# Linear attention and two gated networks on one core: the attention scores always multiplied by the decay on VectorE, straight from PSUM

## The chip, the cores and the metric

The kernel runs on one core of one Trainium2 chip. The metric is the device time of one execution in microseconds (us); lower is better. The engines are written as the profile writes them: PE (TensorE matmul), PEld (TensorE weight load), DVE (VectorE), ACT (ScalarE), POOL (GpSimd) and SP (SyncE, which issues the transfers).

## The reference, cut to what matters

Three stages follow one another. The first is a linear attention over 4 batches, 8 heads and 768 positions, in chunks, with a decay `a` per position:

```python
L = np.exp(cum[:, :, :, None] - cum[:, :, None, :]) * causal   # decay from j to i
CB = np.einsum('bhin,bhjn->bhij', Cc, Bc)                      # scores
M = CB * L                                                     # scores weighed by the decay
y = np.einsum('bhij,bhjd->bhid', M, xc) + y_inter              # y_inter comes from the running state
...
v = k * k @ w_v ;  r = sigmoid(xr @ w_r) ;  x = r * v          # second stage, with k = relu(xk @ w_k)
h = max(x @ w1, x @ w2, x @ w3) ;  out = h @ w_out             # third stage
```

The line `M = CB * L` is the one that the change is about. Here its tile is 128 x 128 per batch, head and block of 128 positions.

## The kernel before, in words

The positions are cut into 6 blocks of 128 (`t`), and the work of a block is: `attention(b, t)` for the 4 batches, then `gate` and `ffn` (the second stage, 512 tokens at a time, block 0 in two halves of 256), then `maxout` and `final` (the third stage). The attentions of block `t + 1` are handed in between `ffn` and `maxout` of block `t`. Large matmuls are made from a high and a low fp32r part of each operand, three products each (`three`, `mm3` at L599). The weights arrive in 64-bit form and are turned into such pairs on the chip, by `load_split` (L549): an absolute value on ACT (L558), four bit operations on DVE (L559 to L565), a copy for the high part (L366/L368) and a subtraction for the low part (L374). All of that falls into the first block.

In `attention(b, t)`, B, C and x are loaded into `bc` and `xt` (L624 to L627), B and C are transposed on PE into a PSUM bank (L641) and copied to `kT` (L645/L646). The decay tile `L` (8 heads x 128 x 128, a ring of two buffers `lr`, `cr` in the code) is loaded as rows by a DMA (L690), masked on POOL (L692) and made into exponentials on ACT (L701, or L697 and L705); for block 0 three of the four batches form it by matmuls (L660 to L684). The scores are made by `cb()` (L708, profile line L712) into four PSUM banks of the pool `pb` (`pa` for the first two batches), 256 columns each. Then they are multiplied by `L` into the SBUF tile `M`, four products of 128 x 256 per attention, 96 in all. At last `yt` (L749) multiplies `M` by x (L761), adds the state's part (L757), and makes the state's update (L752); results go to `xb` (L775/L776) and `st` (L782 to L786).

Each of the 96 products is made by the helper `weigh` (L601). It declares two operations. The first has two choices: DVE multiplies the scores in PSUM by `L` and writes `M` (profile line L604, DVE), or ACT copies the scores from PSUM to `M` (L604, ACT). The second is there only where ACT was chosen: POOL or DVE multiplies `M` by `L` within SBUF (L606).

The order of the work isn't the order of the code. `Plan` holds every operation with its costs by engine and what it depends on. `forward` (L115) goes through time: an engine that is free takes the ready operation with the smallest key. An operation with a choice of engines is put into each engine's queue, into DVE's with `spare` (200 or 1000 ns by turns, `SPARE`) added to its key, and into that of an engine named in `hold` only after so many ns:

```python
                for e in ([late] if late else costs):
                    if not late and e in hold:
                        heapq.heappush(pending, (now + hold[e], i, e))
                        ...
                    heapq.heappush(ready[e], (key[i] - ops[i][4] + (spare if len(costs) > 1 and e == "DVE" else 0.0), i))
```

So ACT gets a copy when DVE hasn't taken the product within 150 ns (`HOLD`). Forty rounds of this are made, with keys from the round before, and the shortest is issued. Each engine then executes its list in that order. Where PE would be idle before the last block-0 matmuls, small matmuls are put in to fill the time (profile line L988).

Of the kernel before, what the change touches and what calls it, by code (L numbers as in the profile page):

```python
# [11 lines left out]
AF = mybir.ActivationFunctionType  # L12
# [43 lines left out]
class Plan:  # L56
# [26 lines left out]
    def op(self, eng, cost, fn, r=(), w=(), after=(), issue=475.0, unless=None, hold=None, tail=0.0, lock=False):  # L83
        deps = set(after)
        for b in r:
            deps.update(b.writers)
        for b in w:
            deps.update(b.readers)
            deps.update(b.writers)
        i = len(self.ops)  # L90
        costs = eng if isinstance(eng, dict) else {eng: cost}
        self.ops.append((costs, fn, sorted(deps), issue, self.bias, unless, hold or {}, tail, lock))
        for b in w:
            b.writers = [i]
            b.readers = []
        for b in r:
            b.readers.append(i)
        return i
# [188 lines left out]

HALVES = (0,)
FIRST = 2
HOLD = 150.0  # L290
HOLD_L = 300.0
HOLD_COPY = 100.0
BIAS = (0.0, 0.0, 0.0)
# [5 lines left out]
def kernel(  # L299
# [20 lines left out]
    P = 128  # L320
# [30 lines left out]
    op = plan.op  # L351
    V, G, A, T, Q = nc.vector, nc.gpsimd, nc.scalar, nc.tensor, nc.sync
# [4 lines left out]
    def tt(n):  # L357
        return 68 + 1.042 * n

    def pool(n, narrow=False):  # L360
        return 147 + (1.95 if narrow else 2.11) * n
# [137 lines left out]
    for s in range(2):  # L499
        hs = halves[s]  # L500
        p = boot.next()
# [3 lines left out]
        p = boot.next()  # L505
# [5 lines left out]
    for s in range(2):  # L511
        p = boot.next()
# [22 lines left out]
    p = boot.next()  # L535
# [62 lines left out]
        for i, (l, r_) in enumerate(terms):  # L598
            T.matmul(pt, l, r_, start=(i == 0), stop=(i == last))  # L599

    def weigh(dst, src, by, n, r, rb, after):  # L601

        i = op({"DVE": tt(n), "ACT": 51 + 0.833 * n}, 0, lambda e: (
            V.tensor_mul(dst, src, by) if e == "DVE" else A.activation(dst, src, AF.Copy)),  # L604
            r=r + [rb], after=after, hold={"ACT": HOLD})
        return op({"POOL": pool(n), "DVE": tt(n)}, 0, lambda e: (V if e == "DVE" else G).tensor_mul(dst, dst, by),  # L606
                  r=[rb], after=[i], unless=(i, "DVE"), lock=True)


    def attention(b, t):  # L610
        ts = slice(t * P, (t + 1) * P)
# [5 lines left out]
        wide = boot if first and b < 2 else pc  # L617
        xb, b_xb = xbs[t % 2], b_xbs[t % 2][b]
        bc, xt, cr = bcr.next(), xtr.next(), lr.next()
# [30 lines left out]
        crg = [Buf(), Buf()]  # L650
        for g in range(2):
            cg = cr.ap[:, 4 * g:4 * g + 4, :]
            cc = ccol[:, qs][:, 4 * g:4 * g + 4, None].to_broadcast([P, 4, P])
            if parts:
                p = wide.next()
# [13 lines left out]
            elif not rows:  # L669
                p = wide.next()  # L670
# [16 lines left out]
            else:  # L687
# [7 lines left out]
                def shift(e, g=g, cg=cg, cc=cc):  # L695
# [3 lines left out]
                    for h in range(4):  # L699
# [3 lines left out]
                i = op({"DVE": tt(512), "POOL": pool(512), "ACT": 4 * 293}, 0, shift, r=[b_cc[b // 2], b_nc[b // 2]],  # L703
                       w=[crg[g]], hold={"ACT": HOLD_L}, lock=True)
# [9 lines left out]
        i = op("PE", 760, cb, r=[kT], w=wide.bufs)  # L714
# [4 lines left out]
        for g in range(2):  # L719
            m = mr.next()  # L720
            ms.append(m)
            base = list(m.readers) + list(m.writers)
            mw = [weigh(m.ap[:, 2 * k:2 * k + 2], wide.bufs[2 * g + k].ap[:, :2 * P].rearrange("p (s i) -> p s i", s=2),
                        cr.ap[:, 4 * g + 2 * k:4 * g + 2 * k + 2], 2 * P, [wide.bufs[2 * g + k]], crg[g], base) for k in range(2)]
            m.writers, m.readers = mw, []
            last.extend(mw)
        cr.readers = last
# [21 lines left out]
        def yt():  # L749
# [9 lines left out]
            for h in range(H):  # L759
# [4 lines left out]
        i = op("PE", (750 if first else 1250) + (170 if more else 0), yt,  # L764
               r=[*ms, xt] + ([] if first else [kT, b_st[b]]) + ([bd] if more else []), w=yb + ([p3] if more else []))
# [7 lines left out]
        base = list(b_xb.readers) + list(b_xb.writers)  # L773
# [4 lines left out]
        if more:  # L778
# [4 lines left out]
            else:  # L783
# [5 lines left out]
                   r=[u, b_dec], w=[b_st[b]], lock=True)  # L789
# [166 lines left out]

    plan.bias = BIAS[1]
    attention(0, 0)
    plan.bias = BIAS[2]
    attention(1, 0)  # L960
    plan.bias = 0.0
    weights_front()
    attention(2, 0)
    attention(3, 0)
    weights_back()
# [56 lines left out]
```

## Time and profile before

| | |
|---|---|
| median of 3 runs | 464.77 us (463.24 to 465.58) |
| the profiled execution's own time | 464.19 us |
| span of the profiled execution | 462.4 us, 8496 instructions |
| PE busy | 439.7 us (95%), 3210 instructions |
| PEld busy | 359.3 us (78%) |
| DVE busy | 287.2 us (62%), 574 instructions |
| ACT busy | 267.3 us (58%), 597 instructions |
| POOL busy | 114.0 us (25%), 140 instructions |
| mean granted TensorE clock | 0.984 of full speed |

The profiled execution's time is its span and 1.79 us around it. Engines work side by side, so their busy times don't add up to the span. A duration of a row is that of one instruction; where a row has several instructions behind one another (x2, x3), its time is that of the whole stretch, which shows at what pace they follow.

### The profile page before, as it was taken

The page shows a single profiled execution, that of the slowest core. Times are in us where ns is not written, and L with a number is a line of the kernel's source. Part 1 is how long each engine was busy: PE and PEld are TensorE (multiplying, and loading weights), DVE is VectorE, ACT ScalarE, POOL GpSimd, SP SyncE. Part 2 cuts the span into 40 slices and gives each one's busy share as a digit, 9 for nine tenths or more (in the row PEclk, how much of TensorE's full clock was granted, in tenths as well). Part 3 has the DMA queues.
Part 4 walks back from the last instruction along what each step waited for, and adds up shares of the span by engine and source line. Part 5 has one row for each costly group of instructions (what it writes and reads, how often), then busy time and mean ns, then how long its engine had stood idle before and what let it go on. Part 6 is the DMA issues. An engine that isn't in the chain of part 4 may idle for free.

```text
span 462.4 us, 8496 instructions
## 1 busy us (share of the span) xinstructions
PE 439.7 (95%) x3210; PEld 359.3 (78%) x3210; DVE 287.2 (62%) x574; ACT 267.3 (58%) x597; POOL 114.0 (25%) x140
## 2 busy tenths in 40 slices
PE   7759899987999999999999999999999999999997
PEld 7648788755887877887877887877888777888887
DVE  5898999979545469635459635459635448423441
ACT  6588999649574454584354584354584433673231
POOL 3022101042024335324335324334322313120000
PEclk9898989999899999999999999999999999999999
DMA  8875636724003342102342102342102400000001
GB/s 220 204 177 115 161 104 163 211 54 87 23 6 71 87 78 59 34 1 62 91 78 58 34 1 62 90 79 59 34 1 51 98 1 0 24 1 23 1 2 45
DMA packets 105705, 31.86 MB, mean 69 GB/s; under 512 B 77632, under 2 KB 101568, under 8 KB 105664
## 3 DMA queue, kind: packets, MB, share of 16 engines
q1 hardware_dynamic: 105664, 31.31, 29.4%
q8 instruction: 25, 0.41, 0.4%
q14 instruction: 16, 0.13, 0.1%
HBM read 27.91 MB, written 3.39 MB: 68 GB/s over the span
## 4 chain that ended last, share of the span: by engine, by line
PE 82%; DVE 7%; ACT 4%; DMA 3%; issue 2%; POOL 1%; SPq 0%; POOLq 0%; ACTq 0%
PE pa L599 47%; PE pa L880 13%; PE pa L936 10%; PE pb L712 2%; PE pb L761 2%; PE pb L641 2%; DMA bc<-in_C_dram 2%; PE pb L757 1%; ACT L L701 1%; DMA L<-crd 1%; PE pb L988 1%; DVE tmp L914 1%; PE pb L936 1%; PE pb L752 1%; DVE tmp L822 1%
## 5 line engine op out<-in xcount | busy, mean ns | idle before, releaser
L914 DVE TENSOR_TENSOR tmp<-tmp,pa 128x512 f32<-128x512 f32 x72 | 49.2, 685 | 45.7 <-PE pa L599 37.4
L374 DVE TENSOR_TENSOR k2l<-tmp,k2h 128x512 fp32r<-128x512 f32 (+1 forms) x48 | 29.1, 610 | 50.6 <-ACT tmp L868 33.8
L692 POOL TENSOR_SCALAR_AFFINE_SELECT L<-L 128x512 f32<-128x512 f32 x40 | 28.8, 740 | 98.5 <-DMA L<-crd 65.2
L936 PE MATMUL pa<-wo,hr 128*128 128x256 f32 x396 | 50.1, 285 | 0.0
L936 PEld LDWEIGHTS pa<-wo,hr 128*128 128x128 f32 x396 | 49.2, 192 | 1.1 <-ACT th L843 0.3
L880 PE MATMUL pa<-k2h,wvh 128*128 128x512 f32 (+1 forms) x112 | 41.8, 373 | 0.0
L366 ACT ACTIVATE hr<-tmp 128x512 fp32r<-128x512 f32 x32 | 20.1, 630 | 37.4 <-DVE tmp L914 37.3
L880 PE MATMUL pa<-k2l,wvh 128*128 128x512 f32 (+1 forms) x112 | 40.3, 360 | 0.0
L866 ACT ACTIVATE k2h<-tmp 128x512 fp32r<-128x512 f32 (+1 forms) x56 | 32.0, 574 | 14.2 <-PE pa L880 13.5
L880 PE MATMUL pa<-k2h,wvl 128*128 128x512 f32 (+1 forms) x112 | 40.2, 359 | 0.0
L865 ACT ACTIVATE tmp<-pa 128x512 f32<-128x512 f32 (+1 forms) x56 | 30.0, 535 | 9.9 <-PE pa L599 9.4
L912 ACT ACTIVATE tmp<-pa 128x512 f32<-128x512 f32 x36 | 21.4, 594 | 17.6 <-PE pa L599 17.3
L604 DVE TENSOR_TENSOR M<-pb,L 128x256 f32<-128x256 f32 x50 | 18.5, 419 | 14.2 <-PE pb L712 14.2
L868 ACT ACTIVATE tmp<-tmp 128x512 f32<-128x512 f32 (+1 forms) x45 | 25.4, 568 | 1.0
L701 ACT ACTIVATE L<-L,ncol 128x128 f32<-128x128 f32 x68 | 21.7, 394 | 5.9 <-POOL L L692 5.9
L374 POOL TENSOR_TENSOR hr<-tmp,hr 128x512 fp32r<-128x512 f32 x14 | 18.3, 1304 | 26.6 <-ACT hr L366 26.4
L880 PEld LDWEIGHTS pa<-k2h,wvh 128*128 128x128 f32 x112 | 21.1, 189 | 4.4 <-issue 1.0
L606 DVE TENSOR_TENSOR M<-M,L 128x256 f32<-128x256 f32 x34 | 23.7, 708 | 0.3 <-ACT M L604 0.2
L880 PEld LDWEIGHTS pa<-k2h,wvl 128*128 128x128 f32 x112 | 21.1, 189 | 3.3
L880 PEld LDWEIGHTS pa<-k2l,wvh 128*128 128x128 f32 x112 | 21.2, 189 | 2.8
L599 PE MATMUL pa<-xk0h,wkh 128*128 128x512 f32 (+1 forms) x56 | 21.9, 391 | 0.9 <-ACT th L843 0.9
L822 DVE SCALAR_TENSOR_TENSOR tmp<-xb,om,tmp 128x512 f32<-128x512 f32 (+1 forms) x28 | 21.7, 800 | 1.2 <-ACT tmp L820 1.0
(230 smaller groups left out, 1135.5 us busy)
## 6 DMA issues: line engine op xcount, KB each, us to landing
L<-crd SPq DMA_DIRECT2D x20, 512.0 KB, 3.8
h<-in_moe_w_dram SPq DMA_DIRECT2D x12, 384.0 KB, 3.4
xt<-in_x_dram SPq DMA_DIRECT2D x24, 128.0 KB, 3.3
out_dram<-outs SPq DMA_DIRECT2D x24, 128.0 KB, 1.7
h<-in_moe_w_k_dram SPq DMA_DIRECT2D x4, 512.0 KB, 5.9
h<-in_moe_w_v_dram SPq DMA_DIRECT2D x4, 512.0 KB, 4.5
bc<-in_B_dram SPq DMA_DIRECT2D x48, 32.0 KB, 2.3
bc<-in_C_dram SPq DMA_DIRECT2D x24, 64.0 KB, 2.8
```

Of the source, the lines that this page charges most:

```text
L374: op({"DVE": tt(n), "POOL": pool(n, narrow)}, 0, lambda e: (V if e == "DVE" else G).tensor_sub(ap(out_), ap(x0), ap(x1)), r=r, w=w, after= ...
L599: T.matmul(pt, l, r_, start=(i == 0), stop=(i == last))
L606: return op({"POOL": pool(n), "DVE": tt(n)}, 0, lambda e: (V if e == "DVE" else G).tensor_mul(dst, dst, by), r=[rb], after=[i], unless=(i, ...
L692: op("POOL", 594, lambda cg=cg: G.affine_select(out=cg, in_=cg, pattern=[[0, 4], [1, P]], compare_op=ALU.is_ge, fill=NEG, base=0, channel_ ...
L701: A.activation(cg[:, h, :], cg[:, h, :], AF.Exp, bias=ncol[:, q:q + 1])
L822: op("DVE", 61 + tt(n), lambda tv=tv, c=c: V.scalar_tensor_tensor(out=tv, in0=xb[:, c, bs, :P], scalar=om[:, i, c:c + 1], in1=tv, op0=ALU. ...
L865: op("ACT", 51 + 0.833 * n, lambda: A.activation(sq, p.ap[:, :n], AF.Relu), r=[p], w=[tm])
L866: op("ACT", act(n), lambda: A.activation(hi, sq, AF.Square), r=[tm], w=[kb])
L868: A.activation(sq, sq, AF.Square) if e == "ACT" else
L880: T.matmul(pv[c2].ap[:, :n], l, r_, start=(f == 0 and i == 0), stop=(f == FC - 1 and i == 2))
L914: op("DVE", tt(TW), lambda p=p, tm=tm: V.tensor_tensor(out=tm.ap, in0=tm.ap, in1=p.ap, op=ALU.max), r=[p], w=[tm])
L936: T.matmul(p.ap[:, c0:c0 + CH], l, r_, start=(g == 0 and i == 0), stop=(g == GC - 1 and i == 2))
```

## The change

The helper `weigh` is gone. Each of the 96 products is one operation, for DVE alone, that reads the scores from PSUM and `L` from SBUF and writes `M`; ACT no longer copies scores, and neither DVE nor POOL multiplies `M` within SBUF. What the operation depends on stays: the bank of scores, the half of `L`, and the earlier users of `M`.

```diff
-HOLD = 150.0
...
-    def weigh(dst, src, by, n, r, rb, after):
-
-        i = op({"DVE": tt(n), "ACT": 51 + 0.833 * n}, 0, lambda e: (
-            V.tensor_mul(dst, src, by) if e == "DVE" else A.activation(dst, src, AF.Copy)),
-            r=r + [rb], after=after, hold={"ACT": HOLD})
-        return op({"POOL": pool(n), "DVE": tt(n)}, 0, lambda e: (V if e == "DVE" else G).tensor_mul(dst, dst, by),
-                  r=[rb], after=[i], unless=(i, "DVE"), lock=True)
...
-            mw = [weigh(m.ap[:, 2 * k:2 * k + 2], wide.bufs[2 * g + k].ap[:, :2 * P].rearrange("p (s i) -> p s i", s=2),
-                        cr.ap[:, 4 * g + 2 * k:4 * g + 2 * k + 2], 2 * P, [wide.bufs[2 * g + k]], crg[g], base) for k in range(2)]
+            mw = [op("DVE", tt(2 * P), lambda g=g, k=k, m=m: V.tensor_mul(
+                m.ap[:, 2 * k:2 * k + 2], wide.bufs[2 * g + k].ap[:, :2 * P].rearrange("p (s i) -> p s i", s=2),
+                cr.ap[:, 4 * g + 2 * k:4 * g + 2 * k + 2]), r=[wide.bufs[2 * g + k], crg[g]], after=base) for k in range(2)]
```

## Rows read from the trace of the kernel before

**Rows 1.** Busy time by stretch: each engine's us and instructions, then PEclk, DMA share, GB/s.

```profile
0.00:24.00 24.00, 18.37 (x208) 16.97 (x209) 17.29 (x48) 14.85 (x34) 4.16 (x21) 0.93 0.87 216
24.00:60.00 36.00, 28.15 (x283) 23.60 (x282) 33.60 (x87) 32.79 (x99) 7.59 (x6) 0.94 0.60 138
60.00:96.00 36.00, 35.31 (x290) 29.71 (x290) 35.20 (x97) 26.61 (x76) 3.51 (x3) 0.97 0.60 156
96.00:116.00 20.00, 14.59 (x124) 9.73 (x124) 16.44 (x34) 16.28 (x45) 5.80 (x8) 1.00 0.38 77
116.00:462.40 346.40, 343.26 (x2311) 279.26 (x2310) 184.64 (x312) 176.81 (x345) 92.91 (x103) 0.99 0.19 42
```

**Rows 2.** Waits of PE, whole span: us in total, times, longest us.

```profile
PE pa L599 <- ACT xr0h L366: 6.3, 3, 3.3
...
PE pb L761 <- DVE M L606: 0.2, 1, 0.2
```

**Rows 3.** Lines L604 and L606 from 0 to 116 us: duration ns min/median/max.

```profile
L604 ACT ACTIVATE M<-pb x14: 362/383/427, 34.7 to 106.4; 128x256 f32<-128x256 f32 x14
L604 DVE TENSOR_TENSOR M<-pb,L x10: 414/422/425, 32.4 to 105.9; 128x256 f32<-128x256 f32 x10
...
L604 ACT ACTIVATE M<-pa x4: 378/381/383, 19.1 to 28.9; 128x256 f32<-128x256 f32 x4
...
L606 DVE TENSOR_TENSOR M<-M,L x18: 411/418/432, 19.8 to 106.8; 128x256 f32<-128x256 f32 x18
```

**Rows 4.** The same two lines from 116 us to the end.

```profile
L604 DVE TENSOR_TENSOR M<-pb,L x40: 415/416/426, 140.7 to 382.6; 128x256 f32<-128x256 f32 x40
L604 ACT ACTIVATE M<-pb x24: 365/378/385, 141.3 to 382.5; 128x256 f32<-128x256 f32 x24
...
L606 DVE TENSOR_TENSOR M<-M,L x16: 416/1050/1349, 141.7 to 382.9; 128x256 f32<-128x256 f32 x16
L606 POOL TENSOR_TENSOR M<-M,L x8: 736/738/868, 155.2 to 362.6; 128x256 f32<-128x256 f32 x8
```

**Rows 5.** The chain that ended last, 24 to 116 us: start, us, what.

```profile
47.26 0.27 ACT M L604
...
87.85 5.72 DMA L<-crd
...
93.73 2.99 POOL L L692
...
106.09 0.39 ACT M L604
```

**Rows 6.** Timeline of ACT, then DVE, 77 to 107 us: start, us, [idle before <-releaser].

```profile
77.60 1.17 ACT L604 ACTIVATE M<-pb 128x256 f32<-128x256 f32 x4
...
82.43 0.42 DVE L606 TENSOR_TENSOR M<-M,L 128x256 f32<-128x256 f32 x1
...
87.03 0.75 DVE L606 TENSOR_TENSOR M<-M,L 128x256 f32<-128x256 f32 x2
...
98.53 0.69 DVE L914 TENSOR_TENSOR tmp<-tmp,pa 128x512 f32<-128x512 f32 x1 [2.32 <-ACT tmp L912]
...
100.25 0.43 DVE L559 TENSOR_SCALAR ms<-ms 128x512 f32<-128x512 f32 x1 [1.03 <-ACT ms L558]
...
105.54 0.76 DVE L604 TENSOR_TENSOR M<-pb,L 128x256 f32<-128x256 f32 x2
...
106.50 0.76 DVE L606 TENSOR_TENSOR M<-M,L 128x256 f32<-128x256 f32 x2 [0.21 <-ACT M L604]
```

**Rows 7.** Timeline of PE, 85 to 115 us.

```profile
85.31 0.60 PE L641 MATMUL pb<-ident,bc 128*128 128x128 f32 x4
...
90.48 0.73 PE L712 MATMUL pb<-kf 32*128 32x128 f32 x16 [0.26 <-DVE u L785]
...
114.62 0.49 PE L599 MATMUL pa<-xr0h,wrh 128*128 128x512 f32 x1 [2.03 <-ACT xr0h L366]
```

**Rows 8.** Busy time by stretch, columns as in rows 1, around 117 us.

```profile
117.00:120.50 3.50, 3.50 (x12) 2.83 (x11) 3.50 (x10) 2.40 (x5) 0.00 (x0) 0.52 0.01 2
```

## The prediction, made before the change was run

> **What bounds the kernel now.** I read busy time by stretch first, to find where PE isn't full; then PE's waits; then the two lines that the change touches, before and after 116 us; then the chain of waits and the timelines where they appear in it.
>
> From 116 us to the end PE is busy for 343.26 of 346.40 us [rows 1]. All idle time of PE there is 3.14 us, and PE's only wait for M in the whole trace is 0.2 us [rows 2]. Two thirds of the products, 40 + 24 of 96, fall into this stretch [rows 4].
>
> Before 116 us things differ. PE is idle for 5.63 us up to 24 us, 7.85 from 24 to 60, 0.69 from 60 to 96 and 5.41 from 96 to 116 [rows 1]: 19.6 us, the room that any change has here. DVE is busy for 33.60 and 35.20 of 36 us in the two middle stretches, and ACT for 32.79 and 26.61: the splitting of the weights goes through both, and DVE is the fuller one. PE's largest wait names what comes out of that work (6.3 us for xr0h) [rows 2]. So the change is worth what it takes off, or puts on, DVE and ACT before 116 us.
>
> **The change part by part.** The sum is made against the profiled execution's own 464.19 us, 0.58 below the median of 464.77.
>
> *Copies on ACT, removed.* 42 in all: 14 + 4 before 116 us [rows 3], 24 after [rows 4]. Four in a row take 1.17 us [rows 6], 0.29 us each, so ACT is relieved of about 18 x 0.29 = 5.3 us in the front and 7.0 us later. The later ones gain nothing: ACT has 169.6 us to spare there [rows 1]. In the front two copies lie on the chain that ended last [rows 5]: 0.27 us at 47.26, where ACT works without a break, and 0.39 us at 106.09, of which DVE waited 0.21 [rows 6]. I take -0.27 - 0.21 = -0.48 us. Bounds for the remaining relief: nothing if DVE stays the limit; and 5.3 / 2 = 2.65 us if every freed microsecond could be shared evenly with DVE. I take nothing, since DVE is the fuller engine in both middle stretches [rows 1].
>
> *Products within SBUF, removed, and products from PSUM, added, on DVE.* Before 116 us 18 SBUF products of 418 ns, one for each copy and all on DVE, give way to 18 PSUM products of 422 ns [rows 3]. Two in a row take 0.76 us in either form [rows 6]. So DVE's load in the front stays: 18 x 0.004 = 0.07 us, taken as 0. [...]
>
> After 116 us, 16 SBUF products on DVE with a median of 1050 ns, and 8 on POOL of 738 ns [rows 4], become 24 of 0.42 us on DVE. DVE gets lighter there, by about 16 x 1.05 - 24 x 0.42 = 6.7 us with the median as the mean, and POOL by 5.9 us. What hides all of this is PE, busy without a break, and DVE's 161.8 idle us [rows 1]. I cost it at 0; were that cover gone, PE's 3.14 idle us bound the gain, and a loss would need DVE to be late, which it is further from than before.
>
> *The banks are held longer.* At 77.60 ACT copied all four scores out of PSUM within 1.17 us; DVE multiplied them between 82.43 and 87.78 [rows 6]. With the change the banks stay taken until DVE comes. Next in line is the transpose of the following attention, at 85.31, which needs one of them; its scores start at 90.48 and wait for a DVE result [rows 7]. If the transpose waited for the last product it would start about 87.8, 2.5 us later, inside those 5.2 us. I take 0; price beyond the slack in the rivals.
>
> *L is given back by the last product.* L has two buffers. The product that ended at 87.78 released the load at 87.85: 5.72 us of transfer, 2.99 us in which POOL masks it [rows 5]. ACT and DVE then stand behind it: DVE idles 2.32 and 1.03 us [rows 6]. No DMA is added or moved in its queue on SP, but its issue follows the product. An earlier product gains at most those 3.35 us of DVE; a later one loses as much as it is late. The code gives both: the product keeps its dependence on L, but as an operation of one engine it loses the `spare` of 200 or 1000 ns on its key, so DVE takes it somewhat earlier, and whatever it overtakes later. I take 0, between a gain of 3.35 and the loss in the second rival, since the rows nearest to it, the 54 products already made in one step on DVE, left PE no wait at all (the 0.2 us are for a product within SBUF) [rows 2].
>
> Sum: 464.19 - 0.48 + 0 = 463.7 us for an execution like the profiled one, and 464.3 us against the median.
>
> **The rivals.** About 0.5%, 2.3 us, is what a measurement of this kernel can tell from no change.
>
> *Forecast, no change:* 462.5 to 467.1, the likeliest value 464.3. For it: DVE's load in the front is the same to 0.07 us, and nothing after 116 us waits for M.
>
> *The L chain moves up (faster).* The products of the attention at 77 us are ready when the copies were (77.60); if DVE made them at once, the reload could leave up to 8 us sooner, and the 3.35 us of DVE idle time near 100 us would be filled: 464.77 - 3.35 - 0.48 = 460.9. For it speaks that DVE had the operands 5 to 9 us before it used them [rows 6]; against it that DVE is full until 96 us [rows 1], so what the four products overtake, weight splitting, comes later by 1.5 us.
>
> *The products overtake what PE waits for (slower).* In the front the products, with no `spare`, go ahead of the mixing and splitting of xr and xk on a full DVE. Four products are 4 x 0.38 = 1.5 us. PE waited for xr0h three times, 2.03 us of it at 112.6 [rows 2, 7]; such a wait grows by 1.5 us wherever four products slip ahead of it. [...] One new place: 1.5 + 1.7 = 3.2 us, 464.3 + 3.2 = 467.5; two such places 470.7. It decides as soon as a mix on which PE already waits lies behind the products. Against it: the plan orders by what ends the span, and sees the mix's need too.
>
> *Nothing is done differently* isn't possible: 42 copies must be gone.
>
> **How the numbers follow.** Forecast 0.50, the slower rival 0.29, the faster one 0.21. [...] The range reaches down to the faster rival's 460.9 and up to 468.8, the slower rival's 467.5 and half of the 2.65 us that the even sharing shows as the size of such shifts; the second break at 470.7 is left out. The forecast's own range is 462.5 to 467.1.
>
> **What the profile would show.** Right: 96 rows of L604's successor on DVE of about 0.42 us, no score copy on ACT, ACT busy 12 to 16 us less (42 x 0.29 or 0.38), POOL 6 us less, PE busy from about 116 us to the end with 3 us idle as now, and the stretch before it within 2 us. The faster rival: the L load near 88 us earlier, and no 2.3 us gap of DVE near 98 us. The slower one: longer waits of PE for xr0h, xk0h or their low parts, and another stretch of half clock. I would be wrong altogether if PE waited for M after 116 us, or if products from PSUM took clearly more than 0.42 us when 96 of them run.

## The result, and the profile after

The changed kernel takes 459.4 us (median of 16 runs, 456.83 to 463.19) against 464.98 us for the kernel before on the same chips. The ratio is 0.9903 with an interval of 0.9874 to 0.9932: faster by 1%, about 4.5 us. It is made from fast runs alone (one execution of the kernel before took 1461.18 us) and isn't the quotient of the two medians, which lie 5.6 us apart. The profiled execution of the changed kernel took 463.19 us, the longest of the 16, with a span of 461.1 us; so a second profiled execution of the same kernel, of span 457.6 us, is shown beside it (it is the run e1 below).

First the busy time by stretch of the changed kernel, columns as in [rows 1].

```profile
0.00:24.00 24.00, 17.22 (x188) 15.64 (x189) 16.54 (x46) 14.48 (x34) 4.57 (x22) 0.85 0.81 209
24.00:60.00 36.00, 30.59 (x283) 26.67 (x283) 32.19 (x87) 30.56 (x90) 4.51 (x5) 0.83 0.62 141
60.00:96.00 36.00, 34.34 (x288) 28.76 (x286) 33.73 (x94) 27.11 (x76) 3.55 (x4) 0.93 0.64 158
96.00:116.00 20.00, 18.14 (x144) 13.21 (x138) 20.00 (x40) 15.36 (x40) 5.29 (x7) 1.00 0.40 78
116.00:461.10 345.10, 341.96 (x2308) 277.88 (x2306) 174.56 (x318) 173.20 (x330) 75.16 (x91) 0.99 0.19 42
```

The same stretches in the second profiled execution:

```profile
0.00:24.00 24.00, 17.67 (x189) 16.02 (x190) 16.99 (x47) 14.80 (x34) 4.62 (x22) 0.89 0.81 211
24.00:60.00 36.00, 30.41 (x288) 25.99 (x287) 33.36 (x90) 31.76 (x93) 4.36 (x5) 0.88 0.66 149
60.00:96.00 36.00, 34.48 (x310) 28.53 (x309) 33.99 (x93) 28.04 (x77) 2.58 (x4) 0.96 0.61 155
96.00:116.00 20.00, 18.36 (x122) 13.76 (x121) 19.94 (x39) 14.60 (x37) 5.68 (x7) 1.00 0.33 66
```

From 116 us to the end nothing has changed for PE: it is idle for 345.10 - 341.96 = 3.14 us, to the hundredth what it was [rows 1]. Ahead of 116 us PE's idle time went from 19.6 us to 15.7 in the one profile and 15.1 in the other. By stretch, before against the second profile: 5.63 to 6.33, 7.85 to 5.59, 0.69 to 1.52, and 5.41 to 1.64. Most of this lies between 96 and 116 us, where DVE went from 16.44 to 19.94 busy us of 20. The small matmuls that fill PE's time count as busy in these rows; all of them lie ahead of 24 us (9.94 us before, 8.29 in the second profile).

The lines that make M, from the view of groups by form (duration ns min/median/max), and the page's first part:

```profile
L714 DVE TENSOR_TENSOR M<-pb,L x88: 408/415/425, 36.5 to 381.6; 128x256 f32<-128x256 f32 x88
...
L714 DVE TENSOR_TENSOR M<-pa,L x8: 415/415/425, 20.3 to 30.4; 128x256 f32<-128x256 f32 x8
```

```profile
PE 442.2 (96%) x3197; PEld 362.1 (79%) x3197; DVE 277.0 (60%) x580; ACT 260.7 (57%) x566; POOL 93.1 (20%) x129
```

All 96 products run on DVE from PSUM (L714, once L604), 0.415 us each, against 0.418 for a product within SBUF in the front [rows 3]. DVE has 10.2 busy us less than before. ACT has only 6.6 less, though 42 copies are gone, and POOL has 20.9 less, though its eight products were 6 us: other operations have moved between the engines.

To tell where the front ends I use a mark that every one of these kernels has in its chain: the first stretch of 36 matmuls of `final` (L936, after the change L928). The chain that ended last, around that mark (start us, us, what): before,

```profile
115.77 4.08 PE pa L599 x11
119.85 4.60 PE pa L936 x36
```

the changed kernel's first profile,

```profile
114.83 4.13 PE pa L598 x11
118.96 4.55 PE pa L928 x36
```

and its second:

```profile
112.65 2.84 PE pa L598 x11
115.49 4.49 PE pa L928 x36
```

From the mark to the end all three have the same left: 462.4 - 119.85 = 342.55, 461.1 - 118.96 = 342.14, 457.6 - 115.49 = 342.11 us. So all but 0.4 us of the result lies ahead of the mark. The eleven matmuls just before it took 4.08, 4.13 and 2.84 us, at a mean granted clock of 0.64, 0.63 and 1.00 of full speed (told of at the end), and the last two are executions of one kernel.

### The profile page after: what moved, and what is told of

The parts are those of the page before. It is cut to its first block, busy times and chain, and to the rows that moved or that the text cites. A ratio compares the mean times of both kernels' runs of the same rounds, so it can differ in the third digit from the quotient of the medians.

```text
span 461.1 us, 8448 instructions
## 1 busy us (share of the span) xinstructions
PE 442.2 (96%) x3197; PEld 362.1 (79%) x3197; DVE 277.0 (60%) x580; ACT 260.7 (57%) x566; POOL 93.1 (20%) x129
## 4 chain that ended last, share of the span: by engine, by line
PE 85%; DVE 7%; ACT 3%; DMA 2%; issue 1%; POOL 0%; SPq 0%; DVEq 0%; ACTq 0%; POOLq 0%
PE pa L598 48%; PE pa L872 13%; PE pa L928 10%; PE pb L703 3%; PE pb L753 2%; PE pb L632 2%; DMA h<-in_moe_w_dram 2%; PE pb L749 1%; DVE M L714 1%; PE pb L928 1%; DVE ms L562 1%; DMA bc<-in_C_dram 1%; PE pb L744 1%; PE pb L980 1%; PE pa L668 1%
## 5 line engine op out<-in xcount | busy, mean ns | idle before, releaser
L683 POOL TENSOR_SCALAR_AFFINE_SELECT L<-L 128x512 f32<-128x512 f32 x40 | 29.0, 745 | 148.4 <-DMA L<-crd 103.8
L928 PEld LDWEIGHTS pa<-wo,hr 128*128 128x128 f32 x396 | 49.2, 192 | 1.1 <-ACT th L835 0.3
L365 ACT ACTIVATE hr<-tmp 128x512 fp32r<-128x512 f32 x36 | 22.6, 632 | 48.3 <-DVE tmp L906 48.3
L928 PE MATMUL pa<-wo,hr 128*128 128x256 f32 x396 | 49.7, 284 | 0.0
L714 DVE TENSOR_TENSOR M<-pb,L 128x256 f32<-128x256 f32 x88 | 31.5, 416 | 1.9 <-PE pb L703 1.9
L692 ACT ACTIVATE L<-L,ncol 128x128 f32<-128x128 f32 x80 | 25.1, 392 | 3.1 <-POOL L L683 3.0
L373 DVE TENSOR_TENSOR hr<-tmp,hr 128x512 fp32r<-128x512 f32 x27 | 18.9, 709 | 11.2 <-ACT hr L365 11.2
L914 ACT ACTIVATE outs<-pa 128x256 f32<-128x256 f32 x22 | 8.4, 383 | 24.7 <-PE pa L928 24.7
L598 PE MATMUL pa<-xk0h,wkl 128*128 128x512 f32 (+1 forms) x56 | 20.7, 369 | 0.0
```

The lines of the kernel that those rows point to most:

```text
L365: A.activation(ap(out_), ap(in_), AF.Copy)
L373: op({"DVE": tt(n), "POOL": pool(n, narrow)}, 0, lambda e: (V if e == "DVE" else G).tensor_sub(ap(out_), ap(x0), ap(x1)), r=r, w=w, after= ...
L683: op("POOL", 594, lambda cg=cg: G.affine_select(out=cg, in_=cg, pattern=[[0, 4], [1, P]], compare_op=ALU.is_ge, fill=NEG, base=0, channel_ ...
L692: A.activation(cg[:, h, :], cg[:, h, :], AF.Exp, bias=ncol[:, q:q + 1])
L714: mw = [op("DVE", tt(2 * P), lambda g=g, k=k, m=m: V.tensor_mul(m.ap[:, 2 * k:2 * k + 2], wide.bufs[2 * g + k].ap[:, :2 * P].rearrange("p ...
L928: T.matmul(p.ap[:, c0:c0 + CH], l, r_, start=(g == 0 and i == 0), stop=(g == GC - 1 and i == 2))
```

## The experiments

Times are medians; ratios are to the kernel before, run beside it on the same chip. "The plan" is the order that `Plan` finds.

### The changed kernel once more (e1)

No edit.

> The changed kernel as it is, for a second profile: the first one is of its slowest execution (463.19 us of 456.83 to 463.19), with a granted clock of 0.83 to 0.85 up to 60 us. If the gain of about 4.5 us comes from the work before 116 us, this profile should show PE starting block 1 (the first matmul of the gate of t = 1 that is followed by work without a break) 3 to 5 us before the 115.8 us of the kernel before, and 346 to 347 us from there to the end in both. If the gain lies after that point, the start should be at 115 to 116 us and the rest some 342 us.

460.5 us, ratio 0.9918 (0.9886 to 0.995). The gain repeats, and the profile above shows a usual execution.

### The copies taken away, the order left as it was (e2, e5)

The plan of before is kept. Where ACT's copy would be issued, DVE's product from PSUM is issued; where the second step would be, nothing.

```diff
-            V.tensor_mul(dst, src, by) if e == "DVE" else A.activation(dst, src, AF.Copy)),
+            V.tensor_mul(dst, src, by)),
...
-        return op({"POOL": pool(n), "DVE": tt(n)}, 0, lambda e: (V if e == "DVE" else G).tensor_mul(dst, dst, by),
+        return op({"POOL": pool(n), "DVE": tt(n)}, 0, lambda e: None,
```

> The plan of the kernel before is made with the helper as it was, and its order is kept; only where it would issue a score copy on ACT, DVE's product straight from PSUM is issued at that place, and the second step is left out. If the work itself is what counts (42 copies off ACT, 42 SBUF products fewer), the time falls by 3 to 5 us, to 460 to 462. If the new order of the whole plan made the gain, the time stays at 463 to 466.

464.57 us, ratio 1.0004 (0.998 to 1.0029): nothing gained, although the same 42 copies and 42 second products are gone as in the change. The reload of L in SP's queue, and the products that give L back, in this run (timelines of SP and DVE):

```profile
91.07 0.44 SPq L557 DMA_DIRECT2D h<-in_moe_w_out_dram  x1
91.61 0.42 SPq L690 DMA_DIRECT2D L<-crd  x1
```

```profile
83.11 0.75 DVE L604 TENSOR_TENSOR M<-pb,L 128x256 f32<-128x256 f32 x2
```

The last product ended at 83.86, and the reload left at 91.61: its place in SP's list was still that of the old order, behind loads of weights whose buffers were not free (SP waited 3.6 us for DVE's `ms` ahead of the one at 90.01). So the products came earlier and the transfer did not. e5 takes that cover away: e2, with the reload put into SP's list 0.3 us behind the last product.

```diff
+        for i in self.reloads:
+            ws = [self.firsts[d] for d in ops[i][2] if d in self.firsts]
+            if ws:
+                start[i] = min(start[i], max(start[d] for d in ws) + 300.0)
```

> The order of e2_frozen_order, products from PSUM at the places of the copies, with one thing moved: each reload of L is put into SP's queue 0.3 us behind the last of the products that give its buffer back, in place of its planned place (in e2 the reload that followed the products done at 83.9 us left only at 91.6, behind weight loads that waited for DVE). If the gain of the change is that L is reloaded earlier, this gives most of it: 460 to 462 us, the reload leaving near 84 to 85 us, DVE without the idle time of 3 us or more between 96 and 108. If something else in the new order made the gain, 464 to 465 as e2.

465.41 us, ratio 1.002 (0.9996 to 1.0044). (`ws` are the products that give the buffer back.) The reload did move, from 91.61 to 81.91 us, and DVE was busy for 19.86 of the 20 us from 96 to 116. Still nothing was gained; the mark stood at 120.43. The idle time had moved to other places: from 60 to 96 us DVE had 33.92 busy us where before had 35.20 [rows 1]. So neither the removed work nor the earlier L makes the gain by itself, while the rest of the order stays.

### The front alone, the rest alone (e3, e4)

The change for `t < 2` only (all products ahead of 116 us), and for `t >= 2` only, each planned anew:

```diff
+            if t < 2:
+                mw = [op("DVE", tt(2 * P), lambda g=g, k=k, m=m: V.tensor_mul(
...
+            else:
+                mw = [weigh(m.ap[:, 2 * k:2 * k + 2],
...
```

> The change for the 8 attentions of blocks 0 and 1 only (32 products), planned anew; the 64 later products keep the helper. If all of the gain lies before 116 us, 459 to 461 us. If it needs the later products too, 463 to 465.

> The change for blocks 2 to 5 only (64 products); the front keeps the helper. If all of the gain lies before 116 us and comes from the products there, 464 to 465 us, as before. If any new plan gains as much by its order, or the later products matter, below 462.

e3: 462.25 us, ratio 0.9951 (0.993 to 0.9973). e4: 464.86 us, 1.0009 (0.9989 to 1.0029). The later 64 products are worth nothing, as was costed. The front alone gives half of the whole, which surprised me: with the later part worth nothing, the front should give all. The orders of e1 and e3 differ in the front too, since every edit has the whole planned anew. That is what the pairs below are for.

### A third buffer for L (e6, e17)

If waiting for L were what held the front, a third buffer should help before, and do nothing more after.

```diff
-    lr = ring("L", 2, [P, H, P])
+    lr = ring("L", 3, [P, H, P])
```

> The kernel before with a third buffer of L, planned anew, copies on ACT and products within SBUF kept. If what the change gains is that L's buffer is given back sooner, a third buffer gains the same without it: 459 to 462 us. If the two-step products themselves cost the time, or the gain is one of a new plan only by chance, it stays at 463 to 466.

> The changed kernel with a third buffer of L, planned anew. If the reload of L still holds up the front without copies, 457 to 458.5 us, below the changed kernel. If the front is DVE's own work by now, 459 to 461, as the changed kernel.

Before with three buffers (e6): 463.38 us, ratio 0.9967 (0.9935 to 0.9999). The changed kernel with three (e17): 464.05 us, ratio 0.9983 (0.9952 to 1.0015), so the gain is nearly lost; there PE waited once for 2.8 us, at its transpose, for a product that held a PSUM bank ("PE pb L632 <- DVE M L714: 2.8, 1, 2.8" among its waits), a wait that the changed kernel doesn't have. The 464.05 lies outside both ranges that were expected. A third buffer gives the kernel before a third of the gain by the middle of its interval, anything from nothing to two thirds by the ends, and since each of the two runs is one order planned anew, they don't show what the wait for a buffer of L is worth.

### The choice kept in the code, ACT never taken (e7)

```diff
-HOLD = 150.0
+HOLD = 1.0e6
```

> The kernel before with its hold for ACT at a million ns: ACT never gets a copy, so that the work is that of the changed kernel, but the product is still an operation with a choice, with the spare of 200 or 1000 ns on its key. If dropping ACT's copy is what counts, 459 to 461 us as the changed kernel. If the missing spare makes the gain (products taken earlier, together), 463 to 465.

459.73 us, ratio 0.9901 (0.9865 to 0.9937), with all 96 products on DVE from PSUM. It keeps the `spare` on the product's key, which the change drops. So the `spare`, which the prediction took for a cause of earlier and overtaking products, isn't the cause of the gain: one constant in the kernel before, which keeps ACT from the copies, gives all of it.

### What a copy in between costs (e8, e9, e13)

All three keep the plan of the changed kernel. e8 makes every second product of `t < 2` (16) in two steps again, at the product's place: ACT copies, DVE multiplies within SBUF.

```diff
+    def weigh2(extra, dst, src, by):
+        if extra:
+            A.activation(dst, src, AF.Copy)
+            V.tensor_mul(dst, dst, by)
+        else:
+            V.tensor_mul(dst, src, by)
```

> The plan of the changed kernel; in 16 of the 32 products of blocks 0 and 1 the instruction is made in two steps after all, a copy on ACT and DVE's product within SBUF, at the product's place in the order (the kernel before had 18 such there). If the order makes the gain, this costs little: the copy ahead of each product, some 0.3 us on the product's way, 460 to 462. If the copies on ACT and the SBUF products cost the time whatever the order, 463 to 465.

465.0 us, ratio 1.0017 (0.9987 to 1.0048): the gain is gone. Busy time by stretch up to the mark, e8 first, then e1 with the same order but for the 16 copies:

```profile
0.00:124.32 124.32, 102.48 (x899) 84.87 (x900) 103.83 (x265) 92.78 (x254) 18.43 (x38) 0.92 0.58 139
```

```profile
0.00:115.49 115.49, 100.42 (x899) 83.79 (x900) 103.78 (x265) 88.89 (x238) 17.25 (x38) 0.93 0.62 150
```

DVE executes the same 265 instructions in the same busy time, 103.8 us; only its idle time grew, from 11.71 to 20.49 us, and the mark moved by the same 8.8 us. These are two single executions, and e8's was the longest of its twelve (468.13 us). By the ratios, 1.0017 against 0.9918, the 16 copies cost 0.0099, or 4.6 us. DVE's waits from 10 to 116 us in e8 (engine line, what it waited for: us in total, times, longest us) name what it stood for:

```profile
DVE M L604 <- ACT M L603: 7.8, 9, 2.1
```

e9 was to part DVE's wait from ACT's load: the copies stay, into a scratch tile that nobody reads, and DVE multiplies from PSUM. e13 does the same with copies of `ident`, a constant in SBUF, in the place of `src`.

```diff
-            A.activation(dst, src, AF.Copy)
-            V.tensor_mul(dst, dst, by)
+            A.activation(pad, src, AF.Copy)
+            V.tensor_mul(dst, src, by)
```

> As e8, but the 16 copies on ACT go to a scratch tile that nobody reads, and DVE multiplies straight from PSUM: ACT has the load of e8, DVE doesn't wait for it. In e8 DVE stood 7.8 us behind ACT's copies and the time was 465.0. If that wait is the price of a score copy, this is near the changed kernel: 459.5 to 461.5. If ACT's load is the price, 463 to 465.

> As e9, but the 16 extra copies on ACT read a constant in SBUF instead of the scores, so that ACT has a like load at the same places and nothing of DVE waits for it. If DVE's wait behind the copy was the price in e8 and e9, 459.5 to 461.5, as the changed kernel. If ACT's load was, 463 to 465.5.

e9: 465.42 us, ratio 1.0018 (0.9988 to 1.0047). It didn't tell the two apart, because DVE waited for the copies all the same:

```profile
DVE M L604 <- ACT pad L603: 4.8, 8, 1.0
```

Copy and product read one PSUM bank, and DVE stood 4.8 us in 8 waits until ACT had made its copy, which nothing reads. This trace shows the wait, not what would come without it.

e13, in which ACT's copies touch nothing that DVE needs and DVE's waits name none of them: 461.44 us, ratio 0.9927 (0.9899 to 0.9955), and in the busy time up to the mark ACT is as full as in e8:

```profile
0.00:114.94 114.94, 98.93 (x899) 81.84 (x900) 104.75 (x265) 93.23 (x254) 18.82 (x38) 0.94 0.62 151
```

So 4.3 us more of ACT in the front (93.23 against 88.89) cost nothing that this measurement can tell: e13's interval covers e1's ratio. What costs is DVE, in order and full, standing before an operand that another engine has still to finish. That price holds for copies put into an order not planned for them. The kernel before, whose plan allows for its copies, shows 0.2 us of such waits up to 116 us, those of [rows 6] at 106.50.

### Other plans of both kernels (e10 to e12, e14 to e16)

Since each edit has the whole order planned anew, part of any difference could be the luck of one order. Three constants of the plan were therefore changed a little, one at a time, in both kernels. They change what the plan reckons with and no line of the work. The first is plan a (e10 before, e11 changed), the second b (e12, e14), the third c (e15, e16).

```diff
-    LAT = {"PE": 230.0, "ACT": 145.0, "DVE": 130.0, "POOL": 90.0}
+    LAT = {"PE": 230.0, "ACT": 145.0, "DVE": 140.0, "POOL": 90.0}
...
-    SPARE = (200.0, 1000.0)
+    SPARE = (300.0, 900.0)
...
-    TO_PE = 260.0
+    TO_PE = 280.0
```

> The kernel before with one number of the planner's estimates changed (130 to 140 ns from DVE to a reader), which gives another order of the same work, score copies still allowed. If the gain is the luck of one order, orders with and without copies overlap, and this may come out anywhere from 459 to 467. If the choice itself makes orders worse, this stays at 463 to 466.

> The changed kernel with the same number changed, another order without copies. If the missing choice makes orders better, 458 to 462, and below e10 by 2 us or more. If it was luck, anywhere from 459 to 467.

> The kernel before with its spare at 300 and 900 ns in place of 200 and 1000: one more order with copies. Choice makes it worse: 463 to 466. Luck: anywhere from 459 to 467.

> The changed kernel with the spare at 300 and 900 ns, the pair of e12 (462.79). Choice makes orders worse: 458 to 461. Luck: anywhere from 459 to 467.

> The kernel before with the planner's latency to PE at 280 instead of 260 ns. Choice makes orders worse: 461 to 466. Luck: anywhere from 459 to 467.

> The changed kernel with the same 280 ns. Choice makes orders worse: 458 to 461, and 2 us or more below e15. Luck: anywhere from 459 to 467.

The ratios, and from the busy time up to the mark (us) DVE's busy time and the rest, its idle time:

| plan | with copies: ratio | mark | DVE busy, idle | without: ratio | mark | DVE busy, idle |
|---|---|---|---|---|---|---|
| as it is | 1 | 119.85 | 106.38, 13.47 | 0.9918 (e1) | 115.49 | 103.78, 11.71 |
| a | 0.9941 (0.9924 to 0.9958) | 117.02 | 104.23, 12.79 | 0.9915 (0.9883 to 0.9947) | 115.75 | 106.11, 9.64 |
| b | 0.9973 (0.9953 to 0.9992) | 118.80 | 108.01, 10.79 | 0.9902 (0.9874 to 0.993) | 115.31 | 105.98, 9.33 |
| c | 0.995 (0.993 to 0.9971) | 118.99 | 109.46, 9.53 | 0.9911 (0.9881 to 0.9941) | 115.37 | 103.64, 11.73 |
| mean | 0.9966 | 118.67 | 107.02, 11.65 | 0.9912 | 115.48 | 104.88, 10.60 |

The row of the kernel before, from which two of these numbers come:

```profile
0.00:119.85 119.85, 100.27 (x911) 83.01 (x912) 106.38 (x271) 93.14 (x258) 21.05 (x37) 0.95 0.60 144
```

Two things are in the table. By the ratio, each of the four orders without copies is faster than each of the four with them; the means differ by 0.0054, or 2.5 us. And the order that the kernel before happens to have is the slowest of its four: a small change of a constant, with all copies kept, gains 0.3 to 0.6%, 1.6 us (0.0034) in the mean. The first is the change's own, as far as four pairs show it; the second is the luck of the order it was measured against. Together they are 0.0088, 4.1 us, near the 4.5 measured.

The split is an estimate. The intervals of plan a overlap; e10 (461.15 us) and e12 (462.79) came out below the 463 that was expected if the choice made orders worse, and e11 is 1.8 us below e10, not the 2 that were asked for. With a third buffer of L the pair is the other way round: 0.9967 with copies (e6), 0.9983 without (e17). And e3, without copies in the front, is at 0.9951 no faster than plan a with them. So an order without copies isn't faster as a rule; these four are.

Where the order of the kernel before loses can be seen at the end of the front. DVE's list around the low part that the eleven matmuls wait for (`xr0l`), before and then in the second profile:

```profile
110.19 0.69 DVE L374 TENSOR_TENSOR wo<-ms,wo 128x512 fp32r<-128x512 f32 x1
...
113.84 0.67 DVE L914 TENSOR_TENSOR tmp<-tmp,pa 128x512 f32<-128x512 f32 x1
114.43 0.68 DVE L374 TENSOR_TENSOR xr1l<-tmp,xr1h 128x512 fp32r<-128x512 f32 x1
115.03 0.68 DVE L374 TENSOR_TENSOR xr0l<-tmp,xr0h 128x512 fp32r<-128x512 f32 x1
115.64 0.68 DVE L374 TENSOR_TENSOR wo<-ms,wo 128x512 fp32r<-128x512 f32 x1
116.24 1.28 DVE L374 TENSOR_TENSOR hr<-tmp,hr 128x512 fp32r<-128x512 f32 x2
```

```profile
111.91 0.68 DVE L373 TENSOR_TENSOR xr0l<-tmp,xr0h 128x512 fp32r<-128x512 f32 x1
112.51 0.68 DVE L373 TENSOR_TENSOR xr1l<-tmp,xr1h 128x512 fp32r<-128x512 f32 x1
113.11 0.68 DVE L906 TENSOR_TENSOR tmp<-tmp,pa 128x512 f32<-128x512 f32 x1
113.71 1.28 DVE L373 TENSOR_TENSOR wo<-ms,wo 128x512 fp32r<-128x512 f32 x2
114.91 1.29 DVE L373 TENSOR_TENSOR hr<-tmp,hr 128x512 fp32r<-128x512 f32 x2
```

In the second profile three operations at a pace of 0.6 us each (`xr1l`, one of `tmp`, one of `wo`) follow `xr0l` that the kernel before has ahead of it: 1.8 us of DVE before what PE waits for. The runs in which this place is as in the kernel before are e2, e4 and e5, whose ratios are 1.0004 to 1.002; in the traces of all other plans, e10, e12 and e15 with their copies among them, five to seven operations follow `xr0l` up to the last `hr`, not three. The size fits the 1.6 us called luck above. No run moves these three alone, so that they are the luck isn't shown.

## Why the prediction was wrong

The sum said 464.3 us and no change; measured were 459.4 us, below the range, which began at 460.9. The step that failed is one that the sum doesn't have: every term was worked out within the order of the kernel before, and the effect of a new order was put at nothing without a reason. Within the old order the sum held: e2, the same work removed there, measures 1.0004 (0.998 to 1.0029), in which the 0.48 us for two copies on the chain can't be told from 0. With the plan free to find another order it is 0.9903.

**The stretch after 116 us, costed at 0: right.** PE's 3.14 idle us are there to the hundredth, and e4, the change for that part alone, measures 1.0009.

**Products from PSUM at no more than those within SBUF: right.** 0.415 us for 96 of them, against 0.418 for the 18 within SBUF [rows 3].

**The banks held longer, costed at 0: right for this kernel.** No transpose (L632 in the second kernel) waits for a product in it. PE's waits for the mixes, the other two rows of before beside [rows 2], and then those of the first profile:

```profile
PE pa L599 <- DVE xr0l L374: 1.3, 2, 0.6
...
PE pa L599 <- ACT xr1h L366: 0.3, 1, 0.3
```

```profile
PE pa L598 <- ACT xr0h L365: 3.0, 2, 2.4
...
PE pa L598 <- DVE xr0l L373: 1.8, 1, 1.8
PE pa L598 <- ACT xr1h L365: 1.8, 1, 1.8
...
PE pa L744 <- DVE M L714: 1.2, 1, 1.2
```

The wait for xr0h has halved, but two others for the same mixes have come beside it: 6.6 us for the three here, 7.9 for the three before (6.3, 1.3 and 0.3). They are not longer, so the slower rival did not come. The one wait for M, 1.2 us, is early, before 31 us. That this term can be other than 0 is seen in e17, with its 2.8 us.

**L given back, costed at 0 between -3.35 and a loss: its signs came, its price isn't shown.** The faster rival's signs are all there. The reload of L and the products before it in the second profile (timelines of SP and of DVE):

```profile
83.90 0.37 SPq L681 DMA_DIRECT2D L<-crd  x1
...
93.97 0.37 SPq L681 DMA_DIRECT2D L<-crd  x1
...
102.82 0.37 SPq L681 DMA_DIRECT2D L<-crd  x1
```

```profile
82.43 1.41 DVE L714 TENSOR_TENSOR M<-pb,L 128x256 f32<-128x256 f32 x4
...
92.51 1.40 DVE L714 TENSOR_TENSOR M<-pb,L 128x256 f32<-128x256 f32 x4
...
101.35 1.41 DVE L714 TENSOR_TENSOR M<-pb,L 128x256 f32<-128x256 f32 x4
```

In the kernel before the second products of one attention were spread from 82.43 to 87.78 [rows 6], with weight splitting between them, and L left at 87.85, 101.07 and 107.33. Now four products follow one another, and L leaves at 83.90, 93.97 and 102.82. DVE's gap of 2.32 and 1.03 us near 100 us [rows 6] is filled. The stretch from 96 to 102 us, before and then in the second profile:

```profile
96.00:102.00 6.00, 4.58 (x45) 2.84 (x45) 2.65 (x7) 3.95 (x11) 2.53 (x3) 1.00 0.00 0
```

```profile
96.00:102.00 6.00, 6.00 (x42) 4.66 (x41) 6.00 (x14) 3.22 (x10) 1.68 (x2) 1.00 0.42 82
```

Those are 2.65 busy us of DVE against 6.00. But the mechanism I gave was too simple. I had it that an earlier product lets L go and the gap closes; e5 did just that in the old order, and nothing was gained. And the late L of 101.07 is a mark of this one order: with copies kept, plans a, b and c send that load at 95.10, 94.61 and 97.55. So the earlier L came with the new order, but no run shows that it made the gain: by e5 it is worth nothing in the old one, and from before to e1 all of DVE's idle time up to the mark fell by 1.76 us, not by 3.35.

**The remaining relief, bounds 0 and 2.65, taken as 0: right for this pair.** I took 0 because DVE was the fuller engine and none of its work went away. DVE's busy time up to the mark does go down, by 2.60 us from before to e1, but the mark cuts DVE's list at two places: from 117.64 to 119.85 us DVE was busy for 2.21 us before, nearly all of it with block 1's next mix, work that e1 has behind its mark. Up to the end of the last `hr` in the two lists above, before and then e1:

```profile
0.00:117.44 117.44, 97.86 (x905) 81.15 (x906) 103.97 (x265) 91.80 (x256) 21.05 (x37) 0.95 0.61 147
```

```profile
0.00:116.12 116.12, 101.05 (x904) 84.42 (x905) 104.41 (x267) 89.32 (x239) 17.25 (x38) 0.93 0.62 149
```

There DVE has not less but 0.44 us more work in e1. Cut at this place, the pairs a, b and c have 0.23, 1.11 and 4.07 us less without copies (104.85 to 104.62, 107.11 to 106.0, 107.87 to 103.8). So some orders do give DVE less to do, but this one doesn't. I had overlooked all the same that the plan shares out more than the products: operations that may go to either engine (copies to `kf` and `xb`, the mixes of L819, the casts to a high part) took 4.0 us of DVE up to the mark before and 3.1 in e1, each summed over its groups; 0.47 of the difference is again a mix behind 117.44 us. By the same sharing ACT has 6.6 us less and POOL 20.9, where I forecast 12 to 16 and 6.

**What was missing, and failed: the plan itself as a cause.** The whole order is planned anew, so any rival can come; the sum gave this no price and no direction. The pairs give both: orders of the same work differ by 0.6% with copies (1 to 0.9941) and by 0.16% without (0.9902 to 0.9918), and an order without the choice is better by 2.5 us in the mean of the four. For the profiles of before and e1 the 4.36 us between the marks can be laid out: the eleven matmuls took 1.24 us less, at a clock of 1.00 against 0.64; DVE's list put three operations, 1.8 us, behind `xr0l`; and DVE came to the end of the last `hr` 1.32 us earlier, 1.76 less idle and 0.44 more busy. The last part is no larger than scatter: in the first profile, the same order, DVE came there at 118.31 us with 13.55 us idle, later than before. A likely reason is that each two-step product ties DVE to the end of a copy on ACT, so that the plan has less freedom and, where its estimates are off, waits; e8's 7.8 us and e10's 3.5 us of DVE waits for copies ("DVE M L606 <- ACT M L604: 3.5, 3, 2.2" among them) point that way. It isn't shown: the waits of e8 were made by hand in an order not planned for them, the kernel before has only 0.2 us of such waits, e3, with no copies in the front, gained just half, and e17, with none at all, almost nothing. Which of the plan's decisions makes the orders with copies worse stays open.

**The chances.** The steps of the sum were each argued within the old order, and then half of the chance was put on no change, 0.21 on the faster side and 0.29 on the slower one. The faster rival's mechanism, an idle DVE near 100 us because L came late, was seen in the profile before; that the result came from it isn't shown. The slower rival's sum has 1.7 us for a low clock behind a new break of PE, a term that no run shows: the eleven matmuls took 4.08 and 4.13 us at a clock of 0.64 and 0.63 and 2.84 at 1.00, which is 1.2 to 1.3 us apart, and in e8 PE waited 1.8 us ahead of them and they took 2.85 all the same.

## What to carry to other kernels

Where a plan makes the order, price an edit over several plans of both kernels (a constant of the planner changed a little), not by one order against one order: here a third of the measured gain, by the mean of four plans, was the luck of the order it was compared with. A step handed to an idle engine is only free if the full engine never has to stand for it: 16 copies of 0.37 us cost 4.6 us in an order not planned for them (e8), and nothing that could be measured when nobody waited for them (e13). And removing the choice can be worth more than removing the work: the same copies taken out of an unchanged order gave nothing.

## What the runs showed of the hardware

The granted clock differed between executions of one kernel. In the kernel before it was 0.52 from 117 to 120.5 us [rows 8], behind a wait of PE of 2.03 us [rows 7]; in the first profile of the changed kernel PE waited 1.75 us at 114.3, and from 115 to 118.9 the clock was 0.62. In the second profile PE waited 1.52 us at 112.1, and it stayed at 1.00 all the way to 119. The same eleven matmuls took 4.08, 4.13 and 2.84 us, so 1.2 to 1.3 us hung on this. The length of that wait alone doesn't account for it: in e8, whose order is that of the first profile but for the copies, PE waited 1.8 us for the same operand (`xr1h`), and yet the clock was 1.00 from 120 to 126 us and the eleven, from 121.47, took 2.85 us. In the first profile the clock was also 0.85 and 0.83 in the first two stretches against 0.93 and 0.94 before [rows 1]. PE was busy for 103.24 us up to the mark there and for 100.42 in the second profile, of the same order (0.89 and 0.88 in the first two stretches). So that execution, with 3.9 us less idle time of PE than before, was only 0.9 us ahead at the mark.

In e2 SP's list in order hid what DVE had gained: the operand of the reload was free at 83.86 us and the transfer was issued at 91.61, 7.75 us later, because other loads ahead of it waited.
